# Convolution by spectra in two channel halves: two products a step, a turned kernel spectrum, sums in the inverse

## Chip, cores and metric

The kernel runs on one NeuronCore of a Trainium2 chip. The metric is the device time of one execution in microseconds. The engines are named as the profile names them: PE (matrix products; PEld is its weight load), DVE and ACT (the two that do elementwise work and empty PSUM), POOL and SP (which mostly issue transfers here). "DMA engines" are the core's 16 transfer engines.

## The reference

Two branches work on the same input x (2048 positions x 640 channels, bf16) and are mixed by a gate. Branch a is attention over 8 positions at stride 2 with 32 heads. Branch b is a long convolution of each channel with a kernel K that a state-space model generates; it is computed by a Fourier transform of length 4096:

```python
P = jnp.exp(logdA[:, :, None] * l[None, None, :])
K = jnp.einsum("dn,dnl,dn->dl", Cc, P, dB).real
Kf = rfft2(pad(K))            # length 2 L
Uf = rfft2(pad(u))
y = irfft2(Uf * Kf)[..., :L] + u * Dskip
...
return g * a + (1 - g) * b    # g = sigmoid((x * gate_w).sum(-1))
```

## The kernel before

The work is written as two plans of tasks, "main" and "tail". A task names the engine or engines that may run it and a duration that a planner assumed; the order in which tasks are issued is not computed when the kernel is built but stands in the strings ORDER["main"] and ORDER["tail"] (read by Plan.order): each entry is a step in the list of tasks, with a letter where the task may run on several engines (A for ACT, D for DVE, S, G for the queues of SP and POOL). Each engine runs its instructions in that order and waits only for semaphores.

**Main** holds the attention (Attn), the generation of K (KGen: arguments on PE, Sin and Exp on ACT, products on DVE, sums on PE) and the first stage of the Fourier transform. K is made in two halves of channels. KExpand spreads a half's result E into the tile X with DVE copies (own, other), stores X to Kx in DRAM and loads it as kc in the layout that the transform wants. The first stage is a matmul with constants: f1 (first half of K, 10 tasks), fu (the input, 20 tasks, from Usb, which rows0 to rows7 load on POOL, each waiting until the one before has landed) and fk (second half of K, five whole tasks and ten half ones, split), each followed by an eviction from PSUM into bufA (K) or big (input).

**Tail** (fft_conv) goes through 32 frequencies f1 in eight steps fb of four. In each step trans computes the real and the imaginary spectrum of K and of the input, all 160 columns x 2 at once with 128x128 weights PHI that hold the same 64x64 block twice: four spectra in two halves h, 8 tasks of four matmuls 128x320, 8 evictions of 128x640 (ACT or DVE, by the order). Then DVE forms the complex product with six operations over 1280 elements: two ta, two tc, and a subtraction and an addition (Y). After all steps the inverse (inv, L1156) multiplies Y by GAB, 20 tiles cp, each of 2 x 8 matmuls of 64 rows in pairs, evicted into C (over bufA). The last stage (fin, L1186) multiplies by psi, and scale, mix or both (L1192 to L1200) add the gated attention gaF, loaded in eight pieces from DRAM by the paced tasks. Eight output tiles are stored by four transfers each, two on SP and two on POOL or, for the last, ACT (L1213).

Of the kernel before, what the change touches and what calls it, by code (L numbers as in the profile page):

```python
# [40 lines left out]
def _attn_consts():  # L41
# [50 lines left out]
), "tail": (  # L92
# [808 lines left out]
class KExpand:  # L901


    def __init__(self, ctx, tc, Dk):
        self.tc, self.nc, self.Dk = tc, tc.nc, Dk
        dr = ctx.enter_context(tc.tile_pool(name="kx_dram", bufs=1, space=DRAM))
        self.Kx = dr.tile([2, 8, 4, KI, 8 * CH], BF16, name="Kx")

    def expand(self, hf, E, pool, psp, S12):
# [18 lines left out]
        def cp(o, i):  # L928
            nc.vector.tensor_copy(o, i)

        def rep(a, h, n):
            return a.unsqueeze(2).to_broadcast([128, h, n, CH])

        def own(_):
            e = E()
            x = X["X"] = pool["kk"].tile([128, 8, 9, CH], BF16, name="X", tag="xkc")
            cp(x[:, 0, 0:8], e[:, 0:8])
            cp(x[:, 1, 0:2], e[:, 13].unsqueeze(1).to_broadcast([128, 2, CH]))
            cp(x[:, 1, 2], e[:, 8])
            cp(x[:, 1, 3:6], e[:, 9].unsqueeze(1).to_broadcast([128, 3, CH]))  # L940
            cp(x[:, 1, 6], e[:, 10])
            cp(x[:, 2:4, 0:3], rep(e[:, 14:16], 2, 3))
            cp(x[:, 2:4, 3:6], rep(e[:, 11:13], 2, 3))
            cp(x[:, 4:8, 0:5], rep(e[:, 16:20], 4, 5))

        def other(_):
            x, nxt = X["X"], X["nxt"]
            cp(x[:, 1, 7], nxt[:, 0])
            cp(x[:, 2:4, 6:8], rep(nxt[:, 1:3], 2, 2))
            cp(x[:, 4:8, 5:9], rep(nxt[:, 3:7], 4, 4))  # L950

        def store(e):
            Kx, x = self.Kx[hf], X["X"]
# [17 lines left out]
def _fft_consts():  # L971
# [11 lines left out]
    phis = np.zeros((64, 2, 32, 3, 2, 64), np.float32)  # L983
    for c2 in range(2):
        phis[:, c2, :, 0, c2, :] = Phi.real.transpose(1, 0, 2)
        phis[:, c2, :, 1, c2, :] = Phi.imag.transpose(1, 0, 2)
        phis[:, c2, :, 2, c2, :] = -Phi.imag.transpose(1, 0, 2)
    phis = phis.reshape(128, 32, 3, 128)
# [3 lines left out]
    gab = np.stack([ga, gb], axis=1)  # L992
    gab = np.concatenate([gab, gab], axis=0).astype(np.float32)
# [9 lines left out]
def fft_prefetch(ctx, tc, x, omS, keep):  # L1003
# [12 lines left out]
    def load_phi(k, eng=nc.gpsimd):  # L1016
        t = pre.tile([128, 4, 3, 128], BF16, name="PHI", tag="PHI", bufs=3)
        eng.dma_start(t[:], phi_d[:, 4 * k:4 * k + 4])
        return t
    P["load_phi"], P["phi_d"] = load_phi, phi_d  # L1020

    def rows(n):
        g, h = n // 2, n % 2
        if n == 0:
            P["Usb"] = pre.tile([128, 64, 160], BF16, name="Usb", tag="uga")
        nc.gpsimd.dma_start(P["Usb"][32 * g:32 * g + 32, 32 * h:32 * h + 32], x.rearrange("(a b) d -> a b d", b=64)[:, 32 * h:32 * h + 32, 160 * BLOCK[g]:160 * BLOCK[g] + 160])
# [19 lines left out]
def fft_conv(ctx, tc, P, big, now, pa, b, gaS, out2d):  # L1046
# [386 lines left out]
```

## Time and profile before

| | us |
|---|---|
| time, median of 3 (lowest, highest) | 314.64 (314.47, 316.12) |
| the profiled execution | 316.68 |
| its span, first to last instruction | 314.9 |
| PE / DVE / ACT busy in the span | 286.3 / 285.9 / 285.2 |
| first fk matmul to last spectrum matmul, start to end | 238.4 to 281.8 |
| inverse, first to last matmul | 283.8 to 295.7 |
| last stage, from its first matmul | 297.0 |

Positions are microseconds from the start of the span. A row of a view gives the engine, the line of the kernel, what is written <- what is read, the tile's shape and a count; "busy" is the time in which at least one instruction of the group ran, so pipelined instructions overlap within it. "L511" is the helper evict on ACT and "L513" the same on DVE; the tiles tell which task it was.

### The profile page before, as it was taken

The page shows a single profiled execution, that of the slowest core. Times are in us where ns is not written, and L with a number is a line of the kernel's source. Part 1 is how long each engine was busy: PE and PEld are TensorE (multiplying, and loading weights), DVE is VectorE, ACT ScalarE, POOL GpSimd, SP SyncE. Part 2 cuts the span into 40 slices and gives each one's busy share as a digit, 9 for nine tenths or more (in the row PEclk, how much of TensorE's full clock was granted, in tenths as well). Part 3 has the DMA queues.
Part 4 walks back from the last instruction along what each step waited for, and adds up shares of the span by engine and source line. Part 5 has one row for each costly group of instructions (what it writes and reads, how often), then busy time and mean ns, then how long its engine had stood idle before and what let it go on. Part 6 is the DMA issues. An engine that isn't in the chain of part 4 may idle for free. (4 is left out here: it accounts for less than half of the span.)

```text
span 314.9 us, 12073 instructions
## 1 busy us (share of the span) xinstructions
PE 286.3 (91%) x5268; PEld 169.8 (54%) x5268; DVE 285.9 (91%) x381; ACT 285.2 (91%) x431; POOL 56.9 (18%) x84
## 2 busy tenths in 40 slices
PE   8799999999999999999999989789999999979740
PEld 3455543444554554555555555447668676659730
DVE  4988999999999989999999999999888899998881
ACT  2789869999999999999999999999989799997890
POOL 8722440302000001111302022020120000000072
PEclk9799999999999999999999999999999999997995
DMA  7995679286111304537795694742493366591076
GB/s 260 363 237 140 183 200 168 81 176 149 24 36 21 106 8 122 108 89 214 192 264 126 127 212 94 153 103 79 169 334 115 131 214 167 113 167 20 4 174 161
DMA packets 47182, 45.70 MB, mean 145 GB/s; under 512 B 27034, under 2 KB 40650, under 8 KB 47130
## 3 DMA queue, kind: packets, MB, share of 16 engines
q1 hardware_dynamic: 40776, 26.68, 32.7%
q0 software_dynamic: 5392, 17.53, 21.7%
q8 instruction: 41, 0.67, 0.9%
q10 hardware_dynamic: 962, 0.73, 0.8%
q14 instruction: 11, 0.09, 0.1%
HBM read 29.60 MB, written 14.01 MB: 138 GB/s over the span
## 5 line engine op out<-in xcount | busy, mean ns | idle before, releaser
L319 PE MATMUL tb<-bufA 128*128 128x512 bf16 x300 | 76.4, 390 | 1.6 <-DMA bufA<-in_A_wqkv_dram 1.2
L842 ACT ACTIVATE big<-ar 128x740 bf16<-128x740 int16 (+1 forms) x72 | 57.6, 876 | 0.2
L827 PE MATMUL ar<-Rarg,L 64*128 64x212 bf16 (+4 forms) x600 | 47.8, 251 | 5.0 <-ACT big L842 2.2
L844 ACT ACTIVATE big<-ar 128x848 bf16<-128x848 f32 x60 | 49.8, 903 | 0.5 <-PE ar L827 0.2
L319 PEld LDWEIGHTS <-bufA 128*128 128x128 bf16 x300 | 31.8, 121 | 30.3 <-issue 9.9
L453 DVE TENSOR_TENSOR pv<-vc,asb 128x2048 bf16<-128x2048 bf16 x40 | 47.7, 1217 | 0.2 <-PE tb L460 0.2
L827 PEld LDWEIGHTS <-L 64*128 64x128 bf16 x600 | 20.7, 94 | 33.7 <-issue 30.8
L864 DVE TENSOR_TENSOR pt<-big 128x1024 bf16<-128x1024 bf16 x48 | 32.2, 702 | 1.5 <-PE kps L882 0.8
L882 PEld LDWEIGHTS <-pt 128*32 128x32 bf16 (+1 forms) x2560 | 23.1, 92 | 11.6 <-issue 9.4
L882 PE MATMUL kps<-qq,pt 128*32 128x21 bf16 (+1 forms) x2560 | 28.1, 174 | 0.6 <-ACT E L511 0.3
L484 PE MATMUL tb<-wo_sb,oT 128*128 128x320 bf16 x160 | 27.7, 301 | 0.9 <-ACT ga L493 0.7
L384 DVE TENSOR_TENSOR prod<-qA,kA 128x2048 bf16<-128x2048 bf16 x20 | 23.8, 1219 | 0.4 <-PE lg L390 0.3
L511 ACT ACTIVATE sp_u<-fp 128x640 bf16<-128x640 f32 x30 | 22.4, 876 | 1.7 <-PE fp L1095 1.7
L384 DVE TENSOR_TENSOR prod<-prj 128x2048 bf16<-128x2048 bf16 x20 | 23.8, 1218 | 0.0
L460 PE MATMUL tb<-pv,ind 128*64 128x512 bf16 (+1 forms) x192 | 22.3, 350 | 0.3 <-DVE pv L453 0.3
L511 ACT ACTIVATE sp_k<-fp 128x640 bf16<-128x640 f32 x30 | 22.2, 883 | 0.4 <-PE fp L1095 0.4
L866 DVE TENSOR_TENSOR qq<-big 128x1344 bf16<-128x1344 bf16 x24 | 21.2, 884 | 0.0
L1213 POOL DMA_DIRECT2D out_dram<-ot x14 | 7.8, 560 | 71.3 <-PE yp L1186 68.8
L1095 PEld LDWEIGHTS <-PHI 128*128 128x128 bf16 x160 | 15.6, 98 | 7.8 <-issue 1.8
L377 POOL DMA_DIRECT2D vc<-vS x16 | 11.5, 726 | 44.5 <-DVE pv L453 39.6
L484 PEld LDWEIGHTS <-oT 128*128 128x128 bf16 x160 | 13.5, 97 | 8.1 <-issue 3.6
L493 ACT ACTIVATE ga<-tb,g_sb 128x320 bf16<-128x320 f32 x28 | 15.2, 570 | 0.0
(171 smaller groups left out, 525.6 us busy)
## 6 DMA issues: line engine op xcount, KB each, us to landing
vc<-vS POOLq DMA_DIRECT2D x16, 327.5 KB, 5.4
gaS<-ga SPq DMA_DIRECT2D x8, 320.0 KB
Usb<-in_A_x_dram POOLq DMA_DIRECT2D x8, 320.0 KB, 5.0
gaF<-gaS SPq DMA_DIRECT2D x8, 320.0 KB
bufA<-in_A_wqkv_dram SPq DMA_DIRECT2D x3, 800.0 KB
L<-Sprm SPq DMA_DIRECT2D x76, 30.0 KB
asb<-aS SPq DMA_DIRECT2D x16, 128.0 KB
psi<-c_psi SPq DMA_DIRECT2D x4, 512.0 KB
```

What stands on the lines that cost most here:

```text
L319: nc.tensor.matmul(ppf, self.wq[:, which, kt, e::5], self.xT[:, c0 // 1024, kt, c0 % 1024:c0 % 1024 + SC], start=(kt == 0), stop=(kt == NK ...
L384: nc.vector.tensor_tensor(b[e][:], q[:, e, o:o + C].unsqueeze(1).to_broadcast([128, W, C]), win(k[:, e, :], o, W, DIL, C), ALU.mult)
L453: nc.vector.tensor_tensor(o, vw, b["asb"][:].unsqueeze(2).to_broadcast(sh), ALU.mult)
L460: nc.tensor.matmul(b["op", e][64 * a:64 * a + 64, 0:n, :], ind[:, 32:96], b["pv", e][:, w, a, 0:n, :], start=(w == 0), stop=(w == 3), skip ...
L484: nc.tensor.matmul(apf[:, :320], b["oT"][:, e, i * 128:(i + 1) * 128], wo_sb[:, e, hf * 320:(hf + 1) * 320], start=(e == 0), stop=(e == 4))
L511: nc.scalar.activation(o, i, ACT.Identity)
L827: nc.tensor.matmul(ar[:, g2, a0:a0 + ncol], L[rows, sb, gv, l0:l0 + 128], R[rows, c0:c0 + ncol], start=True, stop=True, tile_position=(64 ...
L842: nc.scalar.activation(d_[:, :, s0 * QW:s1 * QW], ar[:].bitcast(I16)[:, :, 0:2 * (s1 - s0) * QW:2], ACT.Sin, scale=SCL)
L844: nc.scalar.activation(dst[:, gp::2].rearrange("p g s n -> p g (s n)"), ar[:, :, 0:2 * EW], ACT.Exp)
L864: nc.vector.tensor_tensor(pt[:, :, k, :], gg[:, :, ::-1] if k else gg, e1, ALU.mult)
L866: nc.vector.tensor_tensor(qq[:], trg[:, :, KI:].rearrange("p a (v m) -> p a v m", v=2), exq[:, :, KI:].unsqueeze(2).to_broadcast([128, 32, ...
L882: nc.tensor.matmul(kps[32 * g:32 * g + 32, h, NM * ql:NM * ql + NM], pt[rows, k, v, :], qq[rows, k, v, :], start=(g not in started), stop= ...
```

## The change

The channels are split into two halves hf, and the tail goes through 2 x 8 steps. Data lie in the partitions by a second split c2 (rows 0 to 63 and 64 to 127), so first-stage results are contiguous per frequency, and a matmul of trans has 64 rows and 160 columns; its 128 weight columns give the real spectrum in rows 0 to 63 and the imaginary in rows 64 to 127. The spectrum of K is copied by two SBUF transfers a step (swap) into a tile x with the two 64-row parts exchanged. DVE then forms only two products over 1280 elements: u times k and u times x. Their sums are left to the inverse, whose matmuls now contract all 128 rows (GAB holds the signs).

```diff
 class KExpand:
-        self.Kx = dr.tile([2, 8, 4, KI, 8 * CH], BF16, name="Kx")
+        self.Kx = dr.tile([2, 8, 2, 4 * KI, 4 * CH], BF16, name="Kx")
...
-        def rep(a, h, n):
-            return a.unsqueeze(2).to_broadcast([128, h, n, CH])
+        def rep(o, a, n):
+            for k in range(o.shape[1]):
+                cp(o[:, k], a[:, k].unsqueeze(1).to_broadcast([128, n, CH]))
...
-            cp(x[:, 2:4, 0:3], rep(e[:, 14:16], 2, 3))
-            cp(x[:, 2:4, 3:6], rep(e[:, 11:13], 2, 3))
-            cp(x[:, 4:8, 0:5], rep(e[:, 16:20], 4, 5))
+            rep(x[:, 2:4, 0:3], e[:, 14:16], 3)
+            rep(x[:, 2:4, 3:6], e[:, 11:13], 3)
+            rep(x[:, 4:8, 0:5], e[:, 16:20], 5)
...
-            cp(x[:, 2:4, 6:8], rep(nxt[:, 1:3], 2, 2))
-            cp(x[:, 4:8, 5:9], rep(nxt[:, 3:7], 4, 4))
+            rep(x[:, 2:4, 6:8], nxt[:, 1:3], 2)
+            rep(x[:, 4:8, 5:9], nxt[:, 3:7], 4)
...
-            P["Usb"] = pre.tile([128, 64, 160], BF16, name="Usb", tag="uga")
-        nc.gpsimd.dma_start(P["Usb"][32 * g:32 * g + 32, 32 * h:32 * h + 32], x.rearrange("(a b) d -> a b d", b=64)[:, 32 * h:32 * h + 32, 160 * BLOCK[g]:160 * BLOCK[g] + 160])
+            P["Usb"] = pre.tile([128, 2, 64, 80], BF16, name="Usb", tag="uga")
+        nc.gpsimd.dma_start(P["Usb"][32 * g:32 * g + 32, h], x.rearrange("(a b) d -> a b d", b=64)[:, :, 160 * BLOCK[g] + 80 * h:160 * BLOCK[g] + 80 * h + 80])
...
+    TA = sb.tile([128, 2, 80, 128], BF16, name="TA")
+    gaF = TA[:, 1].rearrange("p z m -> p (z m)").rearrange("p (u d) -> p u d", d=320)
+    ring = {n: [(wa if n != "x" and i < 2 else wk).tile([128, 2, 160, 4], BF16, name=f"sp_{n}{i}") for i in range(w)] for n, w in (("k", 4), ("u", 4), ("x", 4))}
...
+    for n in range(2 * HC):
+        p = ("ar", "fp")[n % 2]
+        fks.append(first("fk", lambda: half[1, "kc"], Bk[:, 1], n, [], [], pl, lambda p=p: bank(p), p))
+    for hf in range(2):
+        for fb in range(8):
+            for nm in "ku":
+                for h in range(2):
+                    p = "ar" if hf or not h else "fp"
...
+                        for fl in range(2):
+                            f1 = 4 * fb + 2 * h + fl
+                            for ri in range(2):
+                                for c2 in range(2):
+                                    r = slice(64 * c2, 64 * c2 + 64)
+                                    nc.tensor.matmul(fp[:, c2, 160 * fl:160 * fl + 160], phis[f1 // 8][r, f1 % 8, 64 - 64 * ri:192 - 64 * ri], B(nm)[r, hf, f1, ri],
+                                                     start=(ri == 0), stop=(ri == 1), skip_group_check=True, tile_position=(64 * c2, 0))
...
+            def swap(_, hf=hf, fb=fb, t=t):
+                t["x"] = ring["x"][(8 * hf + fb) % 4]
+                for i in range(2):
+                    nc.sync.dma_start(t["x"][64 * i:64 * i + 64], t["k"][64 - 64 * i:128 - 64 * i])
...
+                nc.vector.tensor_tensor(o, g("u"), g("kx"[v]), ALU.mult)
+            cuts = ((0, 8), (8, 24), (24, 40)) if hf and fb == 7 else ((0, 40),)
...
+        for cb in range(10):
+            for v in range(2):
...
+                    for l in range(4):
+                        for c2 in range(2):
+                            nc.tensor.matmul(cp[:, c2, l, :], T(hf, v)[:, 40 * c2 + 4 * cb + l], GAB[:, v, :], start=(v == 0 and l == 0), stop=(v == 1), skip_group_check=True)
...
-        for e, t_ in (("S", 0.7), ("G", 1.1) if o < len(TILES) - 1 else ("A", 0.15)):
-            pl.add(f"out{o}{e}", e, t_, store, deps=ends_[o], dma=0.165 * w)
+            pl.add(f"out{o}{i}", "SGA", {"S": 1.42, "G": 1.15, "A": 1.17}, store, deps=ends_[o], dma=0.165 * w)
```

The tasks fk move from the end of main to the head of tail, as ten whole tasks; split goes. The inverse of the first half (inv0..) lies among the spectra of the second (fp1..), and the second half's inverse (inv1..) is the end. Products of the first half go to TA, of the second to big and to Usb's place (TB); gaF takes over half of TA, so its eight loads (paced4 to paced6) wait for the first half's inverse. psi is loaded into kc's place. The rest of the layout changes (bufA, big and C by halves, the constants PHI, GAB) follow from this. Both order strings are new: main is the same for its first 764 of 1264 tasks and ordered anew behind them (rows5 to rows7 now come before the last load of vc, wsin and the last Kx store later), tail throughout. In the new tail the order begins with fk9, fk7, fk0, fp00 and puts 19 of the 64 spectrum evictions, 7 of the 20 of cp and 3 of the 10 of fk on DVE; in its last part it runs, after the first cut of the last products (t0170, t1170), 20 groups of inverse matmuls with 5 evictions and the other cuts on DVE.

More of the change, by code (lines that the diff above doesn't have):

```diff
@@ L982, in _fft_consts @@
     Phi = w(t2[None, :, None] * (f1[:, None, None] + 0.5 + 64 * f2[None, None, :]))
[L983 to L988, printed above, removed]
+    pr, pi = Phi.real.transpose(1, 0, 2), Phi.imag.transpose(1, 0, 2)
+    phis = np.concatenate([np.concatenate([-pi, pr, pi], axis=2)] * 2, axis=0)
     G = np.conj(w(64 * np.outer(f2, t2)))
@@ L1016, in load_phi @@
     def load_phi(k, eng=nc.gpsimd):
-        t = pre.tile([128, 4, 3, 128], BF16, name="PHI", tag="PHI", bufs=3)
-        eng.dma_start(t[:], phi_d[:, 4 * k:4 * k + 4])
+        t = pre.tile([128, 8, 192], BF16, name="PHI", tag="PHI", bufs=3)
+        eng.dma_start(t[:], phi_d[:, 8 * k:8 * k + 8])
         return t
@@ L1045, in fft_conv @@
 @with_exitstack
-def fft_conv(ctx, tc, P, big, now, pa, b, gaS, out2d):
+def fft_conv(ctx, tc, P, big, now, pa, b, gaS, out2d, first, half, kx, kks):
     nc = tc.nc
@@ L1144, in fft_conv @@
-    cps, prev = [], None
-    for cb in range(20):
-        ms = []
-        for ro in range(2):
-            def inv(_, cb=cb, ro=ro):
-                if cb == 0 and ro == 0:
-                    b.close()
-                    q["ps"] = c.enter_context(tc.tile_pool(name="ff_ps3", bufs=4, space=PSUM))
-                if ro == 0:
-                    q["cp", cb] = q["ps"].tile([128, 2, 4, 128], F32, name="cp")
-                for l in range(4):
-                    for c2 in range(2):
-                        nc.tensor.matmul(q["cp", cb][:, c2, l, :], Y[64 * c2:64 * c2 + 64, ro, 4 * cb + l, :],
-                                         GAB[64 * c2:64 * c2 + 64, ro, :], start=(ro == 0 and l == 0), stop=(ro == 1), skip_group_check=True, tile_position=(64 * c2, 0))
-            prev = pl.add(f"inv{cb}{ro}", "P", 0.222, inv, deps=[muls[cb, ro]], after=ends + [prev] + paces, acq=["cy"] if ro == 0 else [])
-            ms.append(prev)
-        def ev(en, cb=cb):
-            evict(nc, en, C.rearrange("p x (c q) -> p x c q", c=2)[:, :, :, 4 * cb:4 * cb + 4], q["cp", cb][:].rearrange("p c l x -> p x c l"))
-        cps.append(pl.add(f"cp{cb}", "AD", {"A": 0.905, "D": 1.13}, ev, deps=ms, rel=[("cy", ms[0])]))
@@ new lines, in psi, with B, TB, T @@
+    def psi(t0, t1):
+        return psx[:, t0 - 44:t1 - 44] if t0 >= 44 else q["psi"][:, t0:t1]
+    def B(nm):
+        return (bufA if nm == "k" else now["big"])[:].rearrange("p (h f r y) -> p h f r y", h=2, f=32, r=2)
+    def TB():
+        if "TB" not in q:
+            q["TB"] = P["pool"].tile([128, 80, 128], BF16, name="TB", tag="uga")
+        return q["TB"]
+    def T(hf, v):
+        return TA[:, v] if hf == 0 else TB()[:] if v else now["big"][:, 0:10240].rearrange("p (z m) -> p z m", m=128)
@@ new lines, in more @@
+    def more(_):
+        phis.append(phx)
+        nc.sync.dma_start(phx[:], phi_d[:, 24:32])
+    early = pl.add("tphi3", "S", 0.7, more, dma=1.6)
+    ends, muls, turned, paces, last, swaps, fks, fus = [], {}, {}, [], None, [], [], []
+    Bk = bufA[:].rearrange("p (h f c q g) -> p h c f q g", h=2, f=64, c=HC, q=8)
+    for n in range(2 * HC):
+        p = ("ar", "fp")[n % 2]
+        fks.append(first("fk", lambda: half[1, "kc"], Bk[:, 1], n, [], [], pl, lambda p=p: bank(p), p))
+    cps, prev, invA = [], None, []
@@ L1263, in gated_mix_kernel @@
     kx = KExpand(ctx, tc, Dk)
-    now = {}
+    now = kx.kk = {}
     def opened():
@@ L1269, in opened @@
             now["big"] = big.enter_context(tc.tile_pool(name="big", side="right", bufs=1)).tile([128, 20480], BF16, name="big")
+            now["kk"] = kks.enter_context(tc.tile_pool(name="kk", side="right", bufs=1))
             kg.open(c2, P["bufA"], now["big"])
-            now["kk"] = c2.enter_context(tc.tile_pool(name="kk", side="right", bufs=1))
     with c2:
@@ L1295, in fetch @@
                 if (hf, "kc") not in half:
-                    half[hf, "kc"] = now["kk"].tile([128, 64, CH], BF16, name="kc", tag="xkc")
+                    half[hf, "kc"] = now["kk"].tile([128, 2, 64, CH // 2], BF16, name="kc", tag="xkc")
                 kx.load(hf, half[hf, "kc"], int(e == "G"), nc.sync if e == "S" else nc.gpsimd)
@@ L1312, in gated_mix_kernel, with first @@
         kg.plan(pl, pa, pk, late[:30] + xdone[-1:], params, opened, fin)
-        def first(name, src, dst, n, deps, after):
+        def first(name, src, dst, n, deps, after, pl=pl, get=lambda: pa.tile([128, 2, 512], F32, name="bp", tag="ar"), tag="ar"):
             b = {}
             def mm(_):
-                sf = src()[:].rearrange("p a b -> p (a b)")
-                st = sf.shape[1] // 128
-                b["bp"] = pa.tile([128, 4, 256], F32, name="bp", tag="ar")
+                sf = src()[:].rearrange("p h t q -> p q (h t)")
+                b["bp"] = get()[:].rearrange("p a (b x) -> p (a b) x", b=2)
                 if name == "fu":
-                    by = b["by"] = b["bp"][:].rearrange("p a (b f) -> p (a b) f", f=64).rearrange("p (g q) f -> p g q f", g=4)
+                    by = b["by"] = b["bp"].rearrange("p a (b f) -> p (a b) f", f=64).rearrange("p (g q) f -> p g q f", g=4)
                     for ql in range(4):
                         for r in range(2):
-                            nc.tensor.matmul(by[:, 2 * r:2 * r + 2, ql], sf[64 * r:64 * r + 64, 4 * n + ql::st], P["F1c"][64 * r:64 * r + 64, 128 * r:128 * r + 128],
+                            nc.tensor.matmul(by[:, 2 * r:2 * r + 2, ql], sf[64 * r:64 * r + 64, 4 * n + ql], P["F1c"][64 * r:64 * r + 64, 128 * r:128 * r + 128],
                                              start=True, stop=True, skip_group_check=True, tile_position=(64 * r, 0))
@@ L1328, in mm @@
                 for ql in range(4):
-                    nc.tensor.matmul(b["bp"][:, ql, :], sf[:, 4 * n + ql::st], P["F1k"][:], start=True, stop=True)
+                    nc.tensor.matmul(b["bp"][:, ql, :], sf[:, 4 * n + ql], P["F1k"][:], start=True, stop=True)
             def ev(en):
                 if name == "fu":
-                    d_ = now["big"][:].rearrange("p (c f q g) -> p c f q g", c=NCH, f=64, q=8)
-                    evict(nc, en, d_[:, n // 2, :, 4 * (n % 2):4 * (n % 2) + 4, :], b["by"].rearrange("p g q f -> p f q g"))
+                    d_ = now["big"][:].rearrange("p (h f c q g) -> p h c f q g", h=2, f=64, c=HC, q=8)
@@ L1340, in first @@
+            m = pl.add(f"{name}{n}", "P", 0.25 if name == "fu" else 0.437, mm, deps=deps, after=after, acq=[tag], eq=1024)
             if name == "f1":
                 half["own"].after.append(m)
-            pl.add(f"{name}e{n}", "AD", {"A": 0.905, "D": 1.13}, ev, deps=[m], rel=[("ar", m)])
-        def split(n, h, deps, after):
-            b = {}
-            def mm(_):
-                sf = half[1, "kc"][:].rearrange("p a b -> p (a b)")
-                st = sf.shape[1] // 128
-                b["bp"] = ps.tile([128, 2, 256], F32, name="tb", bufs=2)
-                for ql in range(2):
-                    nc.tensor.matmul(b["bp"][:, ql, :], sf[:, 4 * n + 2 * h + ql::st], P["F1k"][:], start=True, stop=True)
-            def ev(en):
-                evict(nc, en, Bk[:, HC + n // 2, :, 4 * (n % 2) + 2 * h:4 * (n % 2) + 2 * h + 2, :].rearrange("p f q g -> p f (q g)"),
-                      b["bp"][:].rearrange("p q (g f) -> p f (q g)", f=64))
-            m = pl.add(f"fk{n}h{h}", "P", 0.22, mm, deps=deps, after=after, acq=["tb"], eq=512)
-            pl.add(f"fke{n}h{h}", "AD", {"A": 0.48, "D": 0.60}, ev, deps=[m], rel=[("tb", m)])
+            return pl.add(f"{name}e{n}", "AD", {"A": 0.905, "D": 1.13}, ev, deps=[m], rel=[(tag, m)])
@@ L1369, in gated_mix_kernel @@
         for n in range(2 * HC):
-            first("f1", lambda: half[0, "kc"], Bk, n, half[0, "ld"] + [cst], xdone)
+            first("f1", lambda: half[0, "kc"], Bk[:, 0], n, half[0, "ld"] + [cst], xdone)
         for n in range(2 * NCH):
             first("fu", lambda: P["Usb"], None, n, ub + [cst], kg.pqs)
-        for n in range(2 * HC):
-            if n % 2:
-                for h in range(2):
-                    split(n, h, half[1, "ld"] + [cst], kg.pqs + xdone)
-            else:
-                first("fk", lambda: half[1, "kc"], Bk[:, HC:], n, half[1, "ld"] + [cst], kg.pqs + xdone)
         pl.emit(tc)
-    fft_conv(tc, P, big, now, pa, cp, gaS, o2)
+    fft_conv(tc, P, big, now, pa, cp, gaS, o2, first, half, kx, kks)
 @with_exitstack
```

182 lines of the change are left out of this document (81 added, 101 removed), and 46 rows, old and new, of the table ORDER.

## Prediction

> **What bounds the kernel now.** I read the page's first two parts, then windows of the last third, then the groups by form, the timeline and the waits.
>
> ```profile
> PE 286.3 (91%) x5268; PEld 169.8 (54%) x5268; DVE 285.9 (91%) x381; ACT 285.2 (91%) x431; POOL 56.9 (18%) x84
> ...
> DVE  4988999999999989999999999999888899998881
> ACT  2789869999999999999999999999989799997890
> ```
>
> PE, DVE and ACT are loaded alike; work saved on one helps as far as evictions (which ACT or DVE can do) move there. The windows (duration, then busy time of PE, PEld, DVE, ACT, POOL, granted clock, DMA share, GB/s) cut the end of the kernel into stages.
>
> ```profile
> 238.40:244.70 6.30, 5.43 (x43) 4.68 (x41) 5.98 (x7) 6.07 (x11) 0.00 (x0) 1.00 0.50 154
> 244.70:283.70 39.00, 35.90 (x256) 24.88 (x255) 37.22 (x54) 36.18 (x60) 0.00 (x0) 1.00 0.61 154
> 283.70:297.00 13.30, 11.54 (x320) 10.84 (x321) 12.13 (x18) 11.42 (x12) 0.00 (x0) 0.87 0.05 9
> 297.00:315.00 18.00, 5.77 (x256) 4.64 (x256) 9.16 (x18) 9.32 (x22) 7.75 (x14) 0.81 0.58 148
> 219.70:238.40 18.70, 18.28 (x216) 12.74 (x214) 15.34 (x24) 17.00 (x26) 3.35 (x6) 1.00 0.62 223
> ```
>
> The first three rows are what is rewritten: first stage of the kernel's second half (fk), spectra with products, inverse, one after the other: 58.6 us, in which DVE works 55.3, ACT 53.7, PE 52.9. The fourth is the last stage with the output; the fifth is the end of the main plan, where PE is full and DVE has 3.4 us free.
>
> **The change part by part.** Durations on DVE and ACT, from the timeline (start, duration, count) and one group by form:
>
> ```profile
> 263.40 1.55 DVE L1123 TENSOR_TENSOR ta<-sp_u,sp_k 128x1280 bf16<-128x1280 bf16 x2
> 264.88 1.55 DVE L1123 TENSOR_TENSOR tc<-sp_u,sp_k 128x1280 bf16<-128x1280 bf16 x2
> ...
> 283.01 0.49 DVE L1123 TENSOR_TENSOR tc<-sp_u,sp_k 128x256 bf16<-128x256 bf16 x2
> 283.42 0.49 DVE L1126 TENSOR_TENSOR Y<-ta,tc 128x256 bf16<-128x256 bf16 x2
> 283.82 0.75 DVE L1123 TENSOR_TENSOR tc<-sp_u,sp_k 128x512 bf16<-128x512 bf16 x2
> ```
>
> ```profile
> 288.29 8.49 ACT L511 ACTIVATE bufA<-cp 128x1024 bf16<-128x1024 f32 x9 [0.23 <-PE cp L1156]
> ...
> 291.11 5.74 DVE L513 CAST bufA<-cp 128x1024 bf16<-128x1024 f32 x5
> ```
>
> ```profile
> L513 DVE CAST sp_k<-fp 128x640 bf16<-128x640 f32 x2 | 1.6, 825 | 0.5 <-PE fp L1095 0.5
> ```
>
> *Products.* Two products start 1.48 us before the next two: 0.74 from start to start, 0.08 under one's length. Eight steps of six become 16 steps of two, the last step in three cuts as before: 30 x 0.74 + 2 x (0.41 + 2 x 0.34) = 24.4 us on DVE. Y (L1126), whose writes are strided, runs at the pace of tc, so the new strided writes cost nothing more.
>
> *Evictions.* Still 64 of 128x640, 20 of 128x1024 (cp) and ten of that size for fk. Read off position by position, the new order gives DVE 19, 7 and 3 of them: 19 x 0.745 + 10 x 1.13 = 25.5 us. With the products DVE has 49.9, before 55.3. ACT has 45 x 0.60 (36.18 over 60) + 20 x 0.94 = 45.8, before 53.7. DVE is now clearly the longest; what ACT has free is gain that the order leaves lying.
>
> ```profile
> 292.10:295.70 3.60, 3.53 (x112) 3.22 (x111) 1.00 0.02 5
> ```
>
> ```profile
> 258.30:266.00 7.70, 7.70 (x57) 5.27 (x56) 1.00 0.43 123
> ```
>
> ```profile
> 15.04 1.06 PE L206 MATMUL ar<-ident,xn 128*128 128x128 bf16 x16
> ```
>
> ```profile
> 283.76 8.05 PE L1156 MATMUL cp<-GAB,Y 64*128 64x128 bf16 x208 [1.93 <-DVE Y L1126]
> ```
>
> ```profile
> 284.70:285.70 1.00, 1.00 (x24) 1.00 (x20) 0.89 (x3) 1.00 (x2) 0.00 (x0) 0.50 0.06 13
> ```
>
> *PE.* The first window holds the inverse alone (busy PE, PEld, clock, DMA): 112 matmuls of 64 rows and 128 columns in 3.60 us, 32 ns each. The second holds the spectra: 57 of 320 columns in 7.70 us, 135 ns each, 0.42 a column. At that rate 128 columns take 54 ns, so two 64-row tiles do run side by side. The new spectra are such pairs with 160 columns: 512 x 32 x 160/128 = 20.5 us, before 34.6. The new inverse has 320 matmuls of 128 rows and 128 columns; the L206 row (16 in 1.06, the first 0.22) gives 56 ns, so 17.9 us, before 11.5. With fk's 5.4 PE has 43.8, no bound in the middle. By the Trainium skill (TensorE: Matmul & The Clock Gate, Back-to-back issue gap) a sustained stream of weight loads and 128-column matmuls spaces about 81 ns; by that estimate the inverse takes 25.9 us. The L206 row speaks against it, and it stays as a rival.
>
> *Where DVE stands still.* At the start fk9, fk7 and fp00 must run first: 1.2 us. At the end PE leads: after the first cut of the last products 20 groups of 8 inverse matmuls, 0.45 each, take 9.0 us and the last eviction 1.2; in these 10.2 DVE has four products of 0.34 and 5 x 1.13, 7.0: 3.2 idle. Ahead of that PE waits about 1.5 us for the products; in the last two rows above a gap of 1.93 us was followed by a clock at half. A third of such a loss (1.7 us) is 0.6. Waits in between: 0.6. Sum 49.9 + 1.2 + 3.2 + 0.6 + 0.6 = 55.5 against 58.6, **3.1 us less**. Bounds: 53.5 (no wait in between, no clock loss, a shorter end) and 59.
>
> *Swaps and gaF.* 32 new transfers of 64 rows x 2560 bytes on SP, and behind a waiting second product stand DVE's evictions. No SBUF-to-SBUF transfer is in the trace; the nearest rows are SP's wait for the stores of aS (total, times, longest) and the loads of kc, four times as large (median to landing):
>
> ```profile
> SPq L432 <- DMA aS<-at: 14.6, 5, 4.5
> ```
>
> ```profile
> kc<-Kx POOLq DMA_DIRECT2D x2, 640.0 KB, 8.2
> ```
>
> ```profile
> 279.70:281.90 2.20, 1.87 (x13) 1.07 (x11) 2.20 (x4) 2.20 (x5) 0.00 (x0) 1.00 1.15 235
> 281.90:285.00 3.10, 1.24 (x32) 1.24 (x34) 2.97 (x10) 1.54 (x3) 0.00 (x0) 0.87 0.89 134
> ```
>
> So 2.9 to 8.2 us; I take 3.5, nearest in size. DVE has six operations (3.9 us) between the last step's k evictions and its second product, over 7 us elsewhere: hidden, 0 us. Gone beyond 7, every step waits. gaF can be loaded only when the first half's inverse is done (it takes over TA): the two windows carry its last three loads in 4.7 us of full DMA, so eight take 12.5, against 2.6 + 10.2 + 1.3 = 14 until it is first used. Hidden too, barely; at the other bound 2 us.
>
> *Main plan.* fk leaves it (counted above). own and other get nine more copies per half, and U's loads get shorter runs:
>
> ```profile
> 220.64 1.68 DVE L929 COPY X<-E 128x640 bf16<-128x640 bf16 x8 [0.15 <-PE bp L1329]
> ```
>
> ```profile
> L929 DVE COPY X<-E 128x80 bf16<-128x80 bf16 x4 | 0.7, 176 | 0.0
> ```
>
> ```profile
> 170.69 0.80 POOL L1026 DMA_DIRECT2D Usb<-in_A_x_dram  x1
> ```
>
> ```profile
> 208.07 0.79 POOL L1026 DMA_DIRECT2D Usb<-in_A_x_dram  x1 [3.62 <-DMA Usb<-in_A_x_dram]
> ```
>
> ```profile
> POOL Usb L1026 <- DMA Usb<-in_A_x_dram: 27.3, 5, 6.9
> ```
>
> ```profile
> 203.66:208.00 4.34, 3.68 (x82) 2.09 (x82) 4.30 (x7) 4.33 (x7) 0.79 (x1) 1.00 0.41 94
> ```
>
> ```profile
> 218.10 0.97 PE L1325 MATMUL bp<-F1c,Usb 64*128 64x128 bf16 x16
> ```
>
> The same data is copied, so only the fixed part of a copy counts: 0.10 (the smallest, less the overlap of some 0.07 that makes eight copies 1.68) to 0.18: 0.9 to 1.6 us a half. The first half's lie in DVE's idle time; the second's stand ahead of the Kx store and kc's load, which fk waits for: **+0.9**, bounds 0 and +2.6. U's loads cost nothing while they land before fu needs them (rival C). The rest of the main plan is the same work in another order, with PE full at its end: 0, bounds -1.5 and +1.5.
>
> *Output.* A tile's two pairs of stores may now go by any of three queues.
>
> ```profile
> 306.77 4.08 SPq L1213 DMA_DIRECT2D out_dram<-ot  x6
> ...
> 307.33 1.00 DVE L1200 SCALAR_TENSOR_TENSOR ot<-yp,om,gaF 128x320 bf16<-128x320 f32 x2
> ```
>
> ```profile
> 311.00:312.00 1.00, 0.00 (x0) 0.00 (x0) 0.00 (x0) 0.00 (x0) 0.00 (x0) 0.50 0.87 222
> ```
>
> The last tile is ready at 308.3, SP issues until 310.85; with its last six spread, about 309.7. The DMA engines are near full to 312, so not all of 1.1 us is won: **-0.6**, bounds 0 and -1.2.
>
> Sum: -3.1 + 0.9 - 0.6 = -2.8. The profiled execution has a span of 314.9 (316.68 with what lies around it, 2 us over the median of 314.64); the span should become 312.1 and the median 311.8.
>
> **The rivals.** *A, DVE is kept fed:* it idles 3.3 us as before, the copies hide: -5.4 - 0.6, 308.6. For it: ACT has 9 us to spare. Against: PE leads the end. *B, transfers set the pace:* swaps of 7.2 us make 16 steps wait 0.2, or gaF comes 2 us late: about +3, 314.8. For it: a DMA share of 0.61 in that stage, 1.15 where gaF is loaded. *C, slower, through U's loads:* rows now fetches runs of 160 bytes where it had 320, twice as many, and each load waits for the one before: 0.79 + 27.3/5 = 6.25 us a load. Six (rows2 to rows7) start at about 173 (170.69, and the new order sets some 2.5 us more of DVE work before the buffer that the load ahead of them waits for); fu18 wants the last at about 217.5 (first fu before: 218.10). So 7.4 us a load are to be had. Twice the runs cost between nothing and the DMA time of a load once more, 1.8 us (0.41 of 4.34): 6.25 to 8.05, and more if other queues stretch it. Above 7.4 PE stands at fu18 and all behind it, 6 us for each microsecond a load: at 8.4 +6, or 317.8; over 8.1 the kernel is slower. For it: the count. Against: the last load but one, with little beside it, took 4.4 us (203.66 to 208.07). The Trainium skill (DMA: Bandwidth & Descriptors, Specifications) puts transfers under 512 bytes below line rate, old and new alike; by its cycles per run (Why small descriptors are slow) an estimate is 23% more DMA time, a load of 6.7 us, and C does not come. *D, the weight stream:* 81 ns a matmul make the end's 160 matmuls 4 us longer: 315.8. *E, the 64-row pairs don't pair:* PE would have 41 + 18 + 5 = 64 us and the kernel be slower by 5 or more; the 32 ns of L1156 exclude it.
>
> **How the numbers follow.** Chances: forecast 0.55 (308.8 to 313.0), A 0.12 (down to 306.5), B 0.17 and D 0.03 (313.1 to 316.2), C 0.13 (above). A measurement of this kernel can tell 0.5%, 1.6 us, from no change: faster 0.67, same 0.20, slower 0.13. The range, 307.5 to 316.5, leaves out the lower end of A and most of C, under 0.2.
>
> **What would show it.** DVE near 50 us busy between the first fk and the first yp, and 55 to 56 us from the one to the other; inverse matmuls of 128 rows spaced 56 ns; no idle time of DVE put down to the swaps; U's loads under 7.4 us apart and no wait of PE at the first fu; the last store issued within 1.5 us of the last ot. A stretch above 58 us, or a wait at fu, makes the forecast wrong.

## The result and the profile after

The changed kernel takes 339.38 us (median of 4 runs, 337.44 to 343.94) against 314.87 us: a ratio of 1.075 (95% interval 1.069 to 1.081). The forecast was 311.8. The ratios leave out executions over 1.5% above the fastest of their kernel, at a lower granted clock, and e10 below, whose profile is one of these, has no marks. The profiled execution has a span of 335.2 us in 337.44. The one of the kernel before lies 1.8 us over its median (316.68 against 314.87), and its clock was at half from 284.2 to 287.6 us, in the inverse; the differences of stages below contain that. Three marks cut both executions into the stages of the prediction (us; the last column is counted from the first yp to the end of the span; in the row of the forecast, the first fk is given against before):

| | first fk | fk to first yp | last stage | span |
|---|---|---|---|---|
| before | 238.45 | 58.55 | 17.9 | 314.9 |
| forecast | +0.9 | 55.5 | 17.3 | 312.1 |
| after | 258.65 | 56.78 | 19.8 | 335.2 |

All of the loss lies ahead of the first fk: 20.2 us, in the part of the program that the prediction had called "the same work in another order". The page's first two parts, for the kernel after:

```profile
PE 283.4 (85%) x5496; PEld 172.2 (51%) x5524; DVE 283.4 (85%) x391; ACT 280.8 (84%) x414; POOL 62.2 (19%) x89
...
PE   7899999999999999999875899599981987998740
...
DVE  5989989999999899999947799689980799998491
ACT  2889699999999999999973899789970899897680
```

The engines are busy for as long as before, but three holes have opened: at the 21st to 23rd slice (170 to 190 us), at the 26th (210 to 220) and at the 31st (250 to 258). The windows over the first two, after (columns as in the prediction: duration, busy time of PE, PEld, DVE, ACT, POOL, granted clock, DMA share, GB/s):

```profile
170.00:180.00 10.00, 7.50 (x118) 3.34 (x114) 2.72 (x3) 6.71 (x11) 2.48 (x3) 0.83 1.07 200
180.00:190.00 10.00, 5.97 (x99) 2.91 (x101) 8.89 (x12) 5.00 (x9) 1.91 (x2) 0.66 0.53 108
...
210.00:220.00 10.00, 6.35 (x232) 4.03 (x231) 6.79 (x8) 7.25 (x11) 2.21 (x4) 0.82 0.74 179
```

The chain of waits says on what each hole ended (start, length, what the chain stood on):

```profile
167.32 16.75 DMA gaS<-ga
...
203.88 4.28 DMA aS<-at
...
208.85 5.61 DMA asb<-aS
...
241.93 16.59 DMA kc<-Kx
```

Each is a transfer, and two take over 16 us. The third hole is plain in PE's timeline (start, duration, group, idle time ahead of it and its end):

```profile
258.65 2.76 PE L1336 MATMUL fp<-F1k,kc 128*128 128x256 bf16 x12 [7.83 <-DMA kc<-Kx]
```

The landing of kc, from the list of DMA issues, after (before: 8.2, quoted in the prediction):

```profile
kc<-Kx POOLq DMA_DIRECT2D x2, 640.0 KB, 14.9
```

The windows over kc's second load show what it does to the DMA engines. In the trace's packets nine tenths of what moves in the first row below, from before, are kc, and from 253 to 257 us after, in the third hole, it is all that moves. First before, then after:

```profile
232.00:234.00 2.00, 2.00 (x25) 1.47 (x25) 1.05 (x2) 1.63 (x2) 0.00 (x0) 1.00 0.96 386
```

```profile
254.00:256.00 2.00, 0.00 (x0) 0.00 (x0) 0.00 (x0) 0.00 (x0) 0.00 (x0) 0.50 0.53 120
256.00:258.00 2.00, 0.00 (x0) 0.00 (x0) 0.00 (x0) 0.00 (x0) 0.00 (x0) 0.50 0.46 109
```

Half of the engines work (a share of 0.5 with the load still unfinished), at under a third of the rate. Counted in the trace's packets, 8 of kc are in flight at any time, from 243.5 to 256.5 us, where the kernel before has 16. From 246 to 250.5 us the other half carries packets of PHI beside them, 16 in all; then it runs out of work, and from 253 to 257 us it stands.

**The theory (H).** kc's load takes `Kx[hf]` as `"b h (m w) y -> h b m (w y)"` and picks one h. Rows b and m can't be merged then, since h lies between them, and the slowest dimension of the source has 8 steps; before, all 128 rows were one dimension. A transfer whose slowest dimension has 8 steps would be dealt to 8 engines. By the Trainium skill (DMA: Bandwidth & Descriptors, Why a DMA increments its semaphore by 16 and not by 1) the number of engines is the largest up to 16 that divides the slowest dimension of both sides, here of 8 and 128, so 8; the 8 packets in flight agree. The rivals: the new order of the main plan makes the holes by where it puts stores, late rows and L loads (O); the shorter runs of Kx's store and U's loads fill the engines (R).

### The profile page after: what moved, and what is told of

Its sections match the earlier page's. It is cut to its first block, busy times and chain, and to the rows that moved or that the text cites. A ratio compares the mean times of both kernels' runs of the same rounds, so it can differ in the third digit from the quotient of the medians.

```text
span 335.2 us, 12620 instructions
## 1 busy us (share of the span) xinstructions
PE 283.4 (85%) x5496; PEld 172.2 (51%) x5524; DVE 283.4 (85%) x391; ACT 280.8 (84%) x414; POOL 62.2 (19%) x89
## 4 chain that ended last, share of the span: by engine, by line
PE 38%; ACT 28%; DMA 15%; DVE 10%; issue 6%; SPq 1%; ACTq 0%; DVEq 0%; POOL 0%; POOLq 0%
PE tb L319 11%; PE ar L827 7%; ACT big L844 6%; DMA gaS<-ga 5%; DMA kc<-Kx 5%; ACT big L842 4%; PE tb L484 4%; PE fp L1163 4%; PE kps L882 4%; ACT bufA L511 3%; PE tb L460 3%; PE fp L1107 2%; ACT tt L1200 2%; DMA ident<-c_ident 2%; ACT big L511 2%
## 5 line engine op out<-in xcount | busy, mean ns | idle before, releaser
L319 PE MATMUL tb<-bufA 128*128 128x512 bf16 x272 | 69.3, 382 | 5.2 <-issue 3.4
L842 ACT ACTIVATE big<-ar 128x740 bf16<-128x740 int16 (+1 forms) x72 | 56.9, 862 | 4.5 <-PE ar L827 4.3
L827 PE MATMUL ar<-Rarg,L 64*128 64x212 bf16 (+4 forms) x600 | 48.6, 257 | 3.6 <-ACT big L842 1.5
L844 ACT ACTIVATE big<-ar 128x848 bf16<-128x848 f32 x60 | 50.3, 911 | 0.5 <-PE ar L827 0.4
L484 PE MATMUL tb<-wo_sb,oT 128*128 128x320 bf16 x160 | 29.9, 326 | 3.4 <-ACT ga L493 3.4
L511 ACT ACTIVATE bufA<-fp 128x1024 bf16<-128x1024 f32 x20 | 20.1, 1032 | 14.4 <-PE fp L1336 9.5
L882 PEld LDWEIGHTS <-pt 128*32 128x32 bf16 (+1 forms) x2560 | 22.9, 92 | 17.5 <-issue 13.8
L513 DVE CAST bufA<-fp 128x1024 bf16<-128x1024 f32 x10 | 12.0, 1221 | 10.7 <-PE fp L1336 8.6
L484 PEld LDWEIGHTS <-oT 128*128 128x128 bf16 x160 | 14.4, 103 | 12.7 <-issue 7.1
L493 ACT ACTIVATE ga<-tb,g_sb 128x320 bf16<-128x320 f32 x26 | 14.1, 567 | 5.8 <-DMA gaS<-ga 5.5
L1107 PEld LDWEIGHTS <-PHI 64*128 64x128 bf16 x384 | 14.6, 97 | 7.2 <-issue 6.2
L511 ACT ACTIVATE sp_k<-fp 128x640 bf16<-128x640 f32 x24 | 16.5, 735 | 0.7 <-PE fp L1107 0.6
```

Source lines behind the costliest of these rows:

```text
L319: nc.tensor.matmul(ppf, self.wq[:, which, kt, e::5], self.xT[:, c0 // 1024, kt, c0 % 1024:c0 % 1024 + SC], start=(kt == 0), stop=(kt == NK ...
L484: nc.tensor.matmul(apf[:, :320], b["oT"][:, e, i * 128:(i + 1) * 128], wo_sb[:, e, hf * 320:(hf + 1) * 320], start=(e == 0), stop=(e == 4))
L511: nc.scalar.activation(o, i, ACT.Identity)
L827: nc.tensor.matmul(ar[:, g2, a0:a0 + ncol], L[rows, sb, gv, l0:l0 + 128], R[rows, c0:c0 + ncol], start=True, stop=True, tile_position=(64 ...
L842: nc.scalar.activation(d_[:, :, s0 * QW:s1 * QW], ar[:].bitcast(I16)[:, :, 0:2 * (s1 - s0) * QW:2], ACT.Sin, scale=SCL)
L844: nc.scalar.activation(dst[:, gp::2].rearrange("p g s n -> p g (s n)"), ar[:, :, 0:2 * EW], ACT.Exp)
```

## The experiments

Times are medians of all executions, ratios as above. The kernel before, beside them, had 315.5 for the first four and 314.7 for the others.

| run | time us | ratio to before, 95% | first fk | fk to yp | last stage |
|---|---|---|---|---|---|
| e1_kc16 | 320.60 | 1.013 (1.005 to 1.021) | 240.91 | 55.30 | 21.3 |
| e2_oldmain | 333.12 | 1.053 (1.046 to 1.061) | 251.58 | 59.08 | 21.3 |
| e3_kc16_oldmain | 322.53 | 1.020 (1.012 to 1.028) | 242.74 | 56.40 | 21.4 |
| e4_before_kc8 | 328.99 | 1.040 (1.032 to 1.047) | 250.80 | 59.26 | 17.5 |
| e5_kc16_gaf | 321.32 | 1.019 (1.007 to 1.032) | 241.66 | 56.08 | 19.1 |
| e6_kc16_nogaf | 318.32 | one run | 241.69 | 56.69 | 17.8 |
| e7_hmaj_gaf | 316.34 | 1.005 (1.001 to 1.010) | 238.68 | 58.54 | 19.9 |
| e8_kc16_gaf_early | 318.97 | 1.012 (1.008 to 1.017) | 240.72 | 55.99 | 18.7 |
| e9_hmaj | 318.06 | 1.011 (1.006 to 1.016) | 239.40 | 55.84 | 20.1 |
| e10_hmaj_gaf_early | 316.32 | 1.004 (1.001 to 1.007) | | | |
| e11_hmaj_gaf_psx | 317.37 | 1.008 (1.005 to 1.011) | 241.17 | 54.99 | 18.7 |
| e12_hmaj_gaf_early_psx | 316.40 | 1.002 (0.999 to 1.005) | 238.30 | 55.25 | 19.5 |

The marks come from one profiled execution each. The single runs of the variants scatter more than the differences among e5 to e12 (e12: 314.0 to 321.1), so these are told apart by their stages, and by the time only where the intervals part.

### e1: the same load on 16 engines

```
-  self.Kx[hf].rearrange("b h (m w) y -> h b m (w y)", w=8)[k]
+  self.Kx[hf].rearrange("b h (m w) y -> h m b (w y)", w=8)[k]
-  f1k = ....transpose(1, 0, 2, 3).reshape(128, 256)
+  f1k = ....transpose(1, 0, 2, 3).reshape(8, 16, 256).transpose(1, 0, 2).reshape(128, 256)
```

> The changed kernel with one edit: the rows of kc's load are taken in the order (m, b) in place of (b, m), so that the slowest dimension of the source has 16 steps in place of 8; the constant F1k has its rows in the same order, bytes, runs and instruction order stay. Theory H (half of the DMA engines): the 14.9 us from issue to landing come of the load using 8 of the 16 DMA engines. Then the landing falls to about 8 us as in the kernel before, fk starts some 7 us earlier, the stalls after the first load (170 to 190 us) go, and the time is 315 to 324. Rival O (the new order of the main plan makes the stalls by where it puts the stores, late rows and L loads): the landing of kc stays above 12 us or only the wait at fk goes; 329 or more. Rival R (the runs of 160 and 640 bytes load the DMA engines): nothing moves, 337.

Measured 320.6, 18.8 us less than the change, which had lost 24.5, by the order of two letters. Landing, and the windows of its second load:

```profile
kc<-Kx POOLq DMA_DIRECT2D x2, 640.0 KB, 8.4
```

```profile
234.00:236.00 2.00, 1.96 (x26) 1.44 (x26) 1.77 (x2) 1.61 (x4) 0.00 (x0) 1.00 1.00 248
236.00:238.00 2.00, 2.00 (x26) 1.44 (x28) 1.99 (x3) 1.22 (x2) 0.00 (x0) 1.00 1.07 236
```

The share is 1, and the first fk waits 0.28 us in place of 7.83. The first fu comes at 219.63 where the change had 230.04 (before: 218.10). So of the 17.7 us that the first fk comes earlier, 10.4 belong to what follows the first load of kc, and 7.3 to the second. O and R are left with 2.5 us between them (240.91 against 238.45).

### e2 and e3: the main plan in its old order

The edit puts the steps of the old `ORDER["main"]` (without those of fk) in place of the new ones; e3 has e1's edit too.

> The changed kernel with the main plan in the order of the kernel before (its fk tasks left out, as they stand in the tail now); tail order and all transfers as changed. H: kc's load still takes 14 us or more, so PE waits at f1 and fk as it does in the changed kernel: 330 to 342. O: the stalls at 170 to 190 us go, only the wait for the second kc load stays: 322 to 328. R: as H.

> Both edits: the load on 16 engines and the old main order. H: within 5 us of the first run, 312 to 322. O: this alone comes below 318 while the first run stays at 329 or more. R: 325 or more. The stretch from the first fk to the first yp is the tail alone and was forecast at 55.5 us.

With the 8-engine load the old order still takes 333.1, so the new order doesn't make the holes; it makes them 6 to 7 us worse (339.4 against 333.1, first fk 258.65 against 251.58). With the load mended, the old order has its first fk 1.8 us later than the new one (242.74 against 240.91), and its four runs (322.5 to 322.9) all lie above e1's (318.1 to 321.9). O falls as the cause.

### e4: the kernel before with its load on 8 engines

```
-  self.Kx[hf].rearrange("h g (a b) x -> (h g a) (b x)", a=4)[:, k * w:k * w + w]
+  self.Kx[hf].rearrange("h g (a b) x -> (h g a) (b x)", a=4)[:, k * w:k * w + w].rearrange("(i o) y -> o i y", o=8)
```

F1k's rows are put in the same order.

> The kernel before with the rows of its kc load taken as 8 groups of 16 rows, each group with steps of 8 rows, and F1k's rows to match; nothing else changed. H: kc lands 14 to 16 us after its issue in place of 8.2, PE waits at fk (issue at 228.5, so fk no sooner than 243 against 238.4) and near f1: 8 to 20 us slower, 322 to 335. O and R: unchanged within 1%, 312 to 318.

One line costs the old kernel 13.5 us, and gives it such a hole and such a landing:

```profile
250.80 1.05 PE L1352 MATMUL tb<-F1k,kc 128*128 128x256 bf16 x4 [6.45 <-DMA kc<-Kx]
```

```profile
kc<-Kx POOLq DMA_DIRECT2D x2, 640.0 KB, 15.7
```

```profile
248.00:250.00 2.00, 0.00 (x0) 0.00 (x0) 0.00 (x0) 0.00 (x0) 0.00 (x0) 0.50 0.50 137
```

Together e1 and e4 turn the effect off in one kernel and on in the other. The cause of the loss is shown: it is the pattern of kc's load.

### e5 and e6: the last stage

In e1 the last stage is still 3.4 us longer than before. PE starts yp and then stands; the first sum of DVE that reads gaF comes 4.6 us after the first yp. PE and DVE of e1:

```profile
296.21 1.36 PE L1194 MATMUL yp<-bufA,psi 64*64 64x160 bf16 x66 [1.11 <-ACT bufA L511]
299.26 1.28 PE L1194 MATMUL yp<-bufA,psi 64*64 64x160 bf16 x32 [1.69 <-issue]
```

```profile
300.83 1.01 DVE L1208 SCALAR_TENSOR_TENSOR ot<-yp,om,TA 128x320 bf16<-128x320 f32 x2 [5.13 <-PE yp L1194]
```

DVE's wait is put down to PE, whose matmuls for it were long done; in e9 the same wait carries gaF's name (`[4.72 <-DMA TA<-gaS]`). gaF is loaded from 283.3 on, once the first half's inverse has let go of TA.

```
-  for k in ((), (), (), (), (0, 1), (2, 3, 4), (5, 6, 7))[n]:
+  for k in ((), (), (), (), (0, 2), (4, 6, 1), (3, 5, 7))[n]:      # e5
+  for k in ((), (), (), (), (0,), (), ())[n]:                      # e6
```

> The kernel of e1_kc16 (kc on 16 engines) with the eight loads of gaF in another order: first the four that the first half of the rows needs (k = 0, 2, 4, 6), then the others. Theory G (the last stage of e1_kc16, 21.3 us from the first yp to the end against 17.9 before, is late because the first sums wait for gaF, which loads from 283 to 300 us): the first sum on DVE starts within 2 us of the first yp in place of 4.6, the stage takes 17.5 to 19, the time is 316.5 to 318.5. Rival P (PE's own stall of 1.7 us after 66 matmuls of yp and its clock of 0.5 set the stage): the stage stays at 20.5 or more, 320.

> The kernel of e1_kc16 with seven of the eight loads of gaF left out, so the sums take old values of TA in their place. G: the stage from the first yp to the end falls to 17 to 18 us, and PE's stall after 66 matmuls goes with the transfers that it stands beside. P: the stall and the stage stay, 20 us or more.

PE and DVE of e5, then of e6:

```profile
300.67 0.75 PE L1194 MATMUL yp<-bufA,psi 64*64 64x160 bf16 x32 [1.57 <-issue]
```

```profile
298.60 1.01 DVE L1208 SCALAR_TENSOR_TENSOR ot<-yp,om,TA 128x320 bf16<-128x320 f32 x2 [1.37 <-PE yp L1194]
```

```profile
298.38 2.10 PE L1194 MATMUL yp<-bufA,psi 64*64 64x160 bf16 x98 [1.11 <-ACT bufA L511]
```

With the loads in the order of need DVE starts 0.9 us after the first yp (297.74 to 298.60), and the stage falls from 21.3 to 19.1. PE's stall of 1.6 us stays. Without the loads it goes as well (98 matmuls in one piece), and the stage is 17.8, in a single run. But e5 alone doesn't separate G from P, whose clock of 0.5 is in e1 and not in e5: in e1 the granted clock is at half from 298.6 us to the end, in e5 from 306.6 and in e6 from 307.1 on. Among the profiles whose clock stays up as long, the stage takes 19.8 and 20.1 in the old order (the changed kernel and e9), 18.7 to 19.1 in the order of need (e5, e8, e11) and 17.8 without. By these gaF costs the last stage some 2 us, 0.7 to 1.4 by being late and 0.9 to 1.3 by being under way, and another 1.2 to 1.5 of e1's 21.3 come with its lower clock. What PE stands on is not named by the trace ("issue"); that the stall goes when the loads are left out is shown, that PE's code is held up behind them is only a guess. In the time of the kernel e5's gain is not resolved (320.6 and 321.3, wide intervals).

### e7 and e9: rows that follow one another

e1 reaches a DMA share of 1 but 240 GB/s, where the kernel before has 386. The 8 rows that follow one another in its pattern lie 160 KB apart. These two kernels keep Kx with the channel half outermost:

```
-  self.Kx = dr.tile([2, 8, 2, 4 * KI, 4 * CH], ...)
+  self.Kx = dr.tile([2, 2, 8, 4 * KI, 4 * CH], ...)
-  ... self.Kx[hf].rearrange("b h (m w) y -> h b m (w y)", w=8)[k]
+  ... self.Kx[hf, k].rearrange("b (m w) y -> (b m) (w y)", w=8)
```

The store becomes a loop over h; e7 has e5's order of gaF too.

> The changed kernel with Kx kept with its channel half as the outermost dimension, so that the 128 rows of kc's load lie one behind another as in the kernel before (the store of Kx becomes two transfers for each that was), and with gaF's loads in the order of e5. Theory S (a row's packet of 5120 bytes took 0.36 us in e1_kc16 and 0.23 us in the kernel before because the rows are 160 KB apart there and follow one another here): landing of kc 6 to 7.5 us in place of 8.4, time 0 to 2 us under e5. If the distance of the rows does not matter: as e5, or up to 1 us slower by the six more stores.

> The changed kernel with Kx kept half-major as in e7, so that kc's load is one block of 128 consecutive rows, and nothing else changed (gaF's loads in the order of the change). If the load's pattern is all that the prediction missed ahead of the last stage, the first fk comes at 238 to 239.5, the stretch to the first yp is 55 to 58.5 (the lower end where PE's clock is not cut at the end of the products), the last stage 20 to 21.5 with the wait for gaF: 314 to 318 span, 316 to 320 time. If rows far apart (e1) were as good, 318 to 321 as e1.

Landing and window of e9:

```profile
kc<-Kx POOLq DMA_DIRECT2D x2, 640.0 KB, 6.8
```

```profile
234.00:236.00 2.00, 2.00 (x25) 1.44 (x25) 1.81 (x3) 1.36 (x2) 0.00 (x0) 1.00 1.00 410
```

The rate is back at 410 GB/s with the same 5120-byte packets: the distance of the rows is a second loss inside the first. With it gone the first fk comes at 239.40 and 238.68, near the 238.45 of the kernel before; in e11 below, with the same load, it still comes at 241.17, after a wait of 0.94 us for kc. In the time e9 and e1 can't be told apart (318.1 and 320.6). e7's stretch to the first yp is 58.5: a swap came 1.5 us late, and PE's clock was at half at the head of the inverse. DVE and PE of e7:

```profile
279.42 0.83 DVE L1134 TENSOR_TENSOR TB<-sp_u,sp_x 128x1280 bf16<-128x1280 bf16 x1 [1.52 <-DMA sp_x<-sp_k]
```

```profile
284.91 0.62 PE L1166 MATMUL fp<-GAB,big 128*128 128x128 bf16 x8 [1.68 <-DVE big L1134]
...
286.28 1.02 PE L1166 MATMUL fp<-GAB,big 128*128 128x128 bf16 x8
287.10 1.06 PE L1166 MATMUL fp<-GAB,TB 128*128 128x128 bf16 x8
...
290.59 0.61 PE L1166 MATMUL fp<-GAB,big 128*128 128x128 bf16 x8
```

Eight matmuls take 0.85 us from start to start there and 0.45 later, so the cut costs four groups 1.6 us. What brought it isn't shown: PE stands 1.68 us ahead of the inverse in e3, e6, e8 and e9 too, and there the clock stays up; e7 alone has a gap of 1.22 us as well, 4 us earlier (e9: 0.49). PE of e9:

```profile
285.01 0.62 PE L1166 MATMUL fp<-GAB,big 128*128 128x128 bf16 x8 [1.68 <-DVE big L1134]
285.47 0.62 PE L1166 MATMUL fp<-GAB,TB 128*128 128x128 bf16 x8
```

In e1, e3, e5, e6, e8, e9, e11 and e12 the clock is up over the whole stretch, which takes 55.0 to 56.7.

### e8, e10, e11, e12: trying to get below the kernel before

e8 and e10 move two steps in the main plan's order (the store `xst0G` ahead of `rows0` and `rows1` on GpSimd's queue, these two behind `xld0G`). e11 loads psx with phx at the head of the tail. e12 has all edits.

> e5 with one more edit: on the GpSimd queue the store of the first half of Kx stands ahead of the first two loads of U, and those behind the load of kc. Theory Q (what is left of the main plan's delay, first fk at 240.9 against 238.45, comes of the first kc load being issued at 161.3, 4 us later than before, and colliding with U, vc and L): the first kc load is issued by 155, DVE's wait of 3.0 us at 172 to 175 goes, the time is 1 to 3 us under e5. Rival: the wait of DVE stands for another transfer and nothing moves; as e5 within 1 us.

> e7 (half-major Kx, gaF's loads reordered) with the store of Kx's first half ahead of U's first loads on the GpSimd queue. Theory Q, as for e8 against e5 (a span of 315.4 against 316.8): 0.5 to 2 us under e7, 314 to 316. Rival: as e7 within 0.5, 316.3.

> e7 with the fourth part of psi (640 KB) loaded at the start of the tail in place of at 272 us, between the last swaps. Theory W (in e7 one swap came 1.5 us late at 279 because the psi load and the swaps stood on the engines together; PE's gap after it cost the clock at the inverse: stretch 58.5 in place of 55.3 to 56): no wait of DVE for a swap over 0.7 us, stretch 55 to 56.5, 313.5 to 315.5. Rival (the clock falls after any gap of some 1.7 us at the end of the products, whatever the swaps do): stretch 57 to 59, as e7.

> All four edits together. If Q and W both hold: 312 to 314.5, under the kernel before. If neither: as e7, 316.3.

e8 issues the two halves of the first load at 151.62 and 156.70, where e5 has 160.43 and 160.16, and e5's wait of DVE for vc (2.8 us) is gone, yet the first fk comes only 0.9 us earlier; by the time e8 can't be told from e5 nor e10 from e7. So Q is right about the collision and too high about its worth. In e11 no swap is late by over 0.2 us and the stretch is 55.0, as W asks, but its time is not under e7's, and e9 kept its clock with psi's load where e7 has it (latest swap 0.8 us late), so W's account of e7's clock isn't shown. Its rival, that any gap of some 1.7 us cuts the clock, falls by e9's row above. e12 comes to the time of the kernel before (1.002) and not below it.

## Why the prediction was wrong, step by step

**The step that failed** is the one on the main plan: "The rest of the main plan is the same work in another order, with PE full at its end: 0, bounds -1.5 and +1.5." Within that rest stood the load of kc, whose source pattern the diff changes. The prediction priced the copies ahead of it, but not the load itself; the 8.2 us of the trace of before stand in it only as a bound for the swaps, and that the load keeps them is taken without a word. That term was +20.2 us as measured and +0.2, +0.95 and +2.7 with the load mended in full (e7, e9, e11), against a forecast of +0.9 (-0.15 in e12, which moves a store too). The rule of the Trainium skill named above gives the eight engines from the diff alone; the prediction weighed it nowhere. No rival held it: C looked at U's runs, which didn't matter (U landed in 5.5 us at the median, 5.0 before, and no wait of the first fu was seen; one of U's loads came 11.7 us after the one before, more than C's 7.4, but the first fu itself was late by then). What it had named as signs of being wrong, a stretch above 58 us or a wait at the first fu, did not come; the loss lay where it did not look.

**The stretch from fk to yp** was right: 55.5 forecast, 55.0 to 56.7 in eight profiles with the load mended and the clock up. Not all of the 3.1 us is the change's, though: the 58.6 of before holds a cut of the clock at the inverse, 3.41 us at half, which costs up to 1.7 us (1.6 in e7), and these eight hold none. So the change's own gain there lies between 1.0 and 2.7 us (58.55 against a mean of 55.8, with and without the 1.7); that is an estimate, since before has one profile. The forecast also took its whole 2.8 us off the median, which lies some 2 us below that profile. The row of after, with the clock at half at its start, and of e9:

```profile
258.65:315.43 56.78, 50.44 (x872) 41.88 (x873) 50.32 (x65) 47.68 (x65) 1.87 (x3) 0.95 0.77 183
```

```profile
239.40:295.24 55.84, 48.53 (x874) 40.72 (x873) 51.47 (x66) 48.31 (x66) 1.87 (x3) 1.00 0.78 184
```

DVE has 50.3 and 51.5 us of work (forecast 49.9, before 55.3). ACT has 48 and not 45.8, PE 48.5 and not 43.8; that the sums of pure spacing left out what a group takes to end is a guess, and no run separates it. D falls: eight inverse matmuls start 0.45 us apart, 56 ns each, in e1:

```profile
290.47 0.61 PE L1163 MATMUL fp<-GAB,big 128*128 128x128 bf16 x8
290.92 0.61 PE L1163 MATMUL fp<-GAB,TB 128*128 128x128 bf16 x8
```

By that row the Trainium skill's 81 ns (TensorE: Matmul & The Clock Gate, Back-to-back issue gap) doesn't hold in this stream. E falls by the stretch itself. The swaps are hidden but for waits of 0 to 2.1 us in all.

**The last stage** was mis-sized twice. "Hidden too, barely; at the other bound 2 us" for gaF became some 2 us with the clock up, and 3.5 between e1 and e6: the loads started 13 us ahead of the first yp, as forecast (14), but took some 16 and not 12.5, at 186 GB/s and not 235, beside full engines. The 12.5 was too low by its own rows as well: 2.20 x 1.15 + 3.10 x 0.89 make 5.3 us of full DMA for three loads and not 4.7, so 14 for eight, and no slack was left. In e1:

```profile
290.90:295.90 5.00, 4.20 (x76) 4.10 (x74) 3.58 (x3) 2.60 (x3) 0.00 (x0) 1.00 1.16 186
```

And the -0.6 for spreading the stores over three queues did not come: even without gaF the stage is 17.8, against 17.9 before. From the end of the last ot to the end of the span it is 6.5 us in e6 and 6.6 before. The ACT queue got the last four stores and issued until 312.19 in e6, 2.5 us after the last ot (309.71), as SP did before (310.85 and 308.33), and the DMA engines are as full as before (a share of 1.03 from 310 to 312 us).

**The copies** were +0.4 and not +0.9: from the start of the first copy to the end of the last it takes 3.0 us in e1 (222.12 to 225.12) and 2.6 before (220.64 to 223.22). The store of Kx with its 640-byte runs takes 1.4 us more to the load's issue (224.53 to 231.74 in e1, 222.82 to 228.66 before), which the prediction had not counted.

So with the load mended the change is still no gain: the 1 to 3 us won in the middle go to the last stage (0.8 to 3.5 us longer in the runs with the load mended and all of gaF loaded), where gaF, which gave up its own space, now loads beside the work, and to a first fk that is later in most of them.

## What to carry to other kernels

A change of layout changes every transfer that reads or writes it: write out the access pattern of each, slowest dimension first, and see whether the rows still merge and into how many steps, before taking its duration from the old trace. A DMA share of 0.5 with work outstanding and a chain that stands on transfers of over 10 us is how a load on half of the engines looks, and what else queues behind it (here gaS, aS, asb) pays as well. A buffer that moves into space freed later moves its load later too: work out from what time on it may start, and at which rate beside everything else.

## What the runs showed of the hardware

- A packet of 5120 bytes of kc's second load took 0.20 us at the median in the kernel before (16 engines, rows 10 KB apart) and in e9 (16 engines, rows one behind another), 0.38 in e1 (16 engines, rows 160 KB apart), 0.39 in e4 (8 engines, rows 80 KB apart) and 0.42 after (8 engines, whose shares lie 160 KB apart). So half the engines gave not half but a quarter to a third of the rate. Why the distance matters, no run here shows.
- The two loads of kc, one issued by SP and one by GpSimd, kept together to 8 packets in flight. The other half of the engines took other transfers meanwhile (PHI, 246 to 250.5 us), but none of kc's, and stood free from 253 to 257 us.
- The length of a gap did not settle whether PE's clock was cut. Ahead of the inverse PE stood 1.68 us in e7 and in e9, and the clock was cut in e7 alone; in the last stage it stood 1.37 us in e12 with a cut and 1.78 us in e9 without. In the traces' clock records a cut begins at whole multiples of 3.413 us from any other cut of the same execution, and lasts 3.41, 6.83 or 10.24 us where it ends inside the span. So where the gaps fall on that grid may decide, and the cut in e7 may be chance; that is an inference, since e7 also has the gap of 1.22 us.
